# A hand-written issue list in finer words: recurrent attention and a Fourier mixing layer on one core

## The chip, the cores and the metric

The kernel runs on one core of one Trainium2 chip. A core has five engines that work side by side and wait for each other through semaphores: TensorE (PE in the profile; PEld is its loading of weights), VectorE (DVE), ScalarE (ACT), GpSimd (POOL), and SyncE (SP), which here only issues DMA transfers. The metric is device time in microseconds (us). The kernel before took 525.47 us, the median of three runs (524.52, 525.47, 526.28).

## The reference

A gated recurrent attention ("units" are pairs of heads; 4 batches of 8 heads make 16 units) is followed by a two-dimensional Fourier mixing, a normalisation and a two-layer network. Cut to what is computed:

```python
f = 1 / (1 + exp(-f_logit))                      # (4, 8, 768, 48)
for t in range(768):
    state = f[:, :, t, :, None] * state + einsum('bhd,bhe->bhde', k[:, :, t], v[:, :, t])
    y[:, :, t] = einsum('bhd,bhde->bhe', q[:, :, t], state)
x = y.transpose(0, 2, 1, 3).reshape(4, 768, 384)
mixed = real(fft(fft(x, axis=1), axis=2))
u = x + mixed
un = (u - mean(u)) / sqrt(var(u) + 1e-6)         # over the 384 channels
out = u + maximum(un @ w_ch1, 0) @ w_ch2         # 384 -> 1536 -> 384
```

## The kernel before, in words

**Units.** A unit (two heads, both in one tile of 112 rows and 768 tokens) goes through `attention` and `outputs`. The gates are made into running products inside chunks of 128 tokens: two activations on ACT (lines 372 and 373), a scan on DVE (379, tile `W`), two exponentials on ACT (383, 384), and two products on DVE (391 makes q times the decay, 392 makes k over the decay). PE multiplies keys with queries (400, tile `sc`), DVE masks them (404, tile `at`), PE applies them to the values (559, tile `y`) and makes each chunk's state (599, tile `ds`). DVE chains the states with a scan (607, tile `stt`), PE adds their part to `y` (616), ACT takes `y` out, PE turns it (636, tile `yt`), ACT writes it to `x`. `fold` then makes sums and differences of rows on DVE (663 to 669), and after a batch's last unit those of columns (678 to 687), of which `se` (681) is what the first transform reads first.

**Batches.** When the four units of a batch are folded, `fnet` transforms rows (724, tile `z`, against the table `tab`) and columns (743, tile `mix`, against `cd`), adds and normalises (779, tile `un`; 782 turns it with PE). `projected` multiplies by the first weight matrix (871, tile `up`, in batch 0; 840, tile `ub`, with sums of operands that save products, in the others) and by the second (880, tile `po`, once; 894, tiles `fx` and `fz`, elsewhere).

**Weights.** They arrive as 64-bit floats in 24 pieces (`raw`, three buffers). Each is made a 32-bit float by ACT (281), DVE (283, 284) and POOL (285); POOL's step frees the buffer for the next transfer. At the end `judge` looks at the sizes met and decides whether a slow path has to run (962 to 972, with one product on PE, 969).

**What sets the order.** Nothing is scheduled by a planner. `ORDER` is a list of words, and each word issues one step: a number advances that unit's generator to its next `yield`; F, P and H advance a batch's transforms, its projection and its normalisation; L loads a unit's operands; r fetches a piece of weights, C converts one; V and c reread the weights and look at their sizes; B makes a sum of weights; K turns a unit's keys; M is `judge`; D issues eight 128x128 bf16 products into a spare corner of a PSUM tile that nothing reads (`busy`, line 192). Within an engine, instructions run in the order in which the list issues them, and an instruction that waits holds up all that stand behind it on its engine. The list issues D 21 times.

Of the kernel before, what the change touches and what calls it, by code (L numbers as in the profile page):

```python
# [83 lines left out]
def kernel(  # L84
# [280 lines left out]
    def attention(u, x_all):  # L365
# [18 lines left out]
        nc.scalar.activation(W, W, AF.Exp)  # L384
        te = te_t[u % 2][:R]
# [5 lines left out]
        nc.vector.tensor_tensor(Q, Q, g, ALU.mult)  # L391
        nc.vector.tensor_tensor(g, W, K, ALU.mult)
# [149 lines left out]
    def outputs(u, x_all, AT, Q, K, te, T=None):  # L542
# [26 lines left out]
        if te is not None:  # L569
            own, far = AT  # L570
            diagonal(hi, lo)
            ps = ps_a.tile([128, 2, 512], F32, tag="sc", name=f"sc{u}_1")
            for i in range(NCH // 2):
                for p, c in ((0, i), (64, i + 3)):
                    for r in range(2):
                        nc.tensor.matmul(ps[p:p + 64, r, i * 64:i * 64 + 64],
                                         lhsT=K[ROWS[r], c * C:c * C + 64],
                                         rhs=Q[ROWS[r], c * C + 64:(c + 1) * C], start=True, stop=True)
            nc.scalar.copy(far, ps[:, :, :NCH // 2 * 64].rearrange("p r (c t) -> p r c t", t=64))
            yield  # L580
# [6 lines left out]
        else:  # L587
# [4 lines left out]
            diagonal(lo, hi)  # L592
        ps = ps_a.tile([128, 2, 512], F32, tag="sc", name=f"ds{u}")
# [21 lines left out]
        for c, r in ((1, 0), (4, 1), (4, 0), (1, 1), (2, 0), (3, 1), (3, 0), (2, 1), (5, 0), (5, 1)):  # L615
            nc.tensor.matmul(y[ROWS[into(c, r)], c // 3, c % 3 * C:c % 3 * C + C], lhsT=st[ROWS[r], :, c - 1],  # L616
                             rhs=Q[ROWS[r], c * C:(c + 1) * C], start=False, stop=True,
                             skip_group_check=True)

# [15 lines left out]
        for c, i in enumerate((0, 1, 4, 2, 3, 5)):  # L635
            nc.tensor.transpose(ps[:, c * 128:c * 128 + R], to[:, i], ident[:R, :R])  # L636
        x = x_all()
# [9 lines left out]
    def fold(u, x):  # L647
# [16 lines left out]
        tt(f[:, 1:4], x[:, 0:3, ch], x[:, 3:6, ch], ALU.add)  # L664
        tt(f[:, 0:8:7], f[:, 1:7:5], f[:, 2:6:3], ALU.add)
# [13 lines left out]
        if last:  # L679
            eo_of.pop(b)  # L680
            tt(se[:, :, 1:QD], xs[:, :, 1:QD], xs[:, :, HD - 1:QD:-1], ALU.subtract)
            tt(xs[:, :, 1:QD + 1], xs[:, :, 1:QD + 1], xs[:, :, HD - 1:QD - 1:-1], ALU.add)
        tt(xc[:, :, lo:hi], eo[:, 0:4, lo:hi], eo[:, 0:4, up], ALU.add)
# [18 lines left out]
    def fnet(b, x):  # L702
# [71 lines left out]
        def turn(c):  # L774
# [4 lines left out]
            nc.vector.tensor_scalar(un, x[:, c], mv[:, c, 0:1], rstd[:, c:c + 1], ALU.subtract, ALU.mult)  # L779
            pt = ps_f.tile([128, 512], F32, tag="f", name=f"pt{b}_{c}")  # L780
# [4 lines left out]
        def turns():  # L785

            for step in ((0, [3], 3, [4, 5], 2, 5, 1, 4) if b < B - 1 else ([4, 5], 2, 5, [3], 1, 3, 0, 4)):
# [4 lines left out]
                else:  # L792
                    turn(step)
# [3 lines left out]
        for c in range(3):  # L797
            mix = mixed(c)
            nc.vector.tensor_tensor(by2(x[:, c]), rising(mix, NQ), by2(x[:, c]), ALU.add)
            moments(c)  # L800
            deviation(slice(c, c + 1))
            nc.vector.tensor_tensor(by2(x[:, c + 3]), falling(mix, NQ), by2(x[:, c + 3]), ALU.add)
# [311 lines left out]
```

## Time and profile before

| | |
|---|---|
| median of 3 runs | 525.47 us |
| profiled execution, span | 526.3 us (526.257 in the trace) |
| PE busy | 494.9 us, 94% |
| DVE busy | 378.3 us, 72% |
| ACT, POOL busy | 218.4 us, 58.8 us |
| first product of the first transform (line 724) | 59.54 us |
| last piece of weights converted on DVE (line 284) | 117.00 us |
| last product of the program starts and ends | 517.32 us, 519.43 us |

The span is the time from the first to the last instruction of one execution. A row of a timeline gives start, length, engine, line, operation, tiles (out<-in), shape, how many instructions are merged in it, and in brackets the idle time before it with what ended it. PE's busy time has the pipeline's overlap in it, so products are better judged by the distance between their starts.

### The profile page before, as it was taken

The numbers are of one execution on the slowest core, as the hardware profiler recorded it, in microseconds if no ns is written. First come the engines' busy times: TensorE is split into PE (matmuls) and PEld (weight loads), VectorE is DVE, ScalarE is ACT, GpSimd is POOL, SyncE is SP. The second block draws the span as 40 slices with busy tenths as digits, with TensorE's granted clock in tenths as the row PEclk, the third lists the DMA queues.
The fourth block names the chain that finished last, engine by engine and source line by source line (L and its number), as shares of the span: only waits on it lengthen the run. The fifth ranks groups of instructions, "written<-read, shape, count | busy, mean of one in ns | idle before, by whom it ended". The sixth has DMA issues, their size and how long they took to land.

```text
span 526.3 us, 13807 instructions
## 1 busy us (share of the span) xinstructions
PE 494.9 (94%) x5854; PEld 453.4 (86%) x5854; DVE 378.3 (72%) x746; ACT 218.4 (42%) x520; POOL 58.8 (11%) x85
## 2 busy tenths in 40 slices
PE   5878599999999999999999999999999999999994
PEld 4757388866899889999999999999999999999994
DVE  3598989989955368688588776779776667465571
ACT  5567368656331542453435523550431404031220
POOL 3045033551001000000001000000001000010100
PEclk9789699999999999999999999999999999999998
DMA  8957837575010230103212012120610312220200
GB/s 222 268 147 206 210 109 214 161 221 158 6 55 30 68 97 17 54 21 114 77 55 84 1 55 72 46 63 23 206 43 15 107 47 81 83 91 8 84 11 27
DMA packets 20650, 48.15 MB, mean 91 GB/s; under 512 B 3426, under 2 KB 6179, under 8 KB 20579
## 3 DMA queue, kind: packets, MB, share of 16 engines
q1 hardware_dynamic: 19474, 43.63, 29.5%
q0 software_dynamic: 1104, 3.54, 1.8%
q8 instruction: 48, 0.79, 0.6%
q14 instruction: 24, 0.19, 0.1%
HBM read 42.44 MB, written 4.72 MB: 90 GB/s over the span
## 4 chain that ended last, share of the span: by engine, by line
PE 87%; DVE 6%; issue 2%; ACT 2%; DMA 1%; POOL 0%; SPq 0%; DVEq 0%; ACTq 0%
PE ub L840 23%; PE fx L894 16%; PE fz L894 11%; PE up L871 9%; PE z L724 5%; PE y L559 4%; PE mix L743 3%; PE y L616 2%; PE sc L400 2%; PE ds L599 2%; PE po L880 2%; PE yt L636 2%; PE pt L782 1%; PE st L538 1%; PE y L192 1%
## 5 line engine op out<-in xcount | busy, mean ns | idle before, releaser
L849 DVE TENSOR_TENSOR h<-h,ub 128x512 f32<-128x512 f32 x81 | 55.2, 687 | 33.5 <-PE ub L840 24.5
L692 POOL DMA_INDIRECT out_dram<-x,place x16 | 16.4, 1024 | 357.6 <-DVE x L944 224.3
L847 ACT ACTIVATE h<-ub 128x512 f32<-128x512 f32 x54 | 31.9, 591 | 42.3 <-PE ub L840 42.3
L871 PE MATMUL up<-unT,w 128*128 128x256 f32 x216 | 49.4, 382 | 0.0
L840 PE MATMUL ub<-wide,w 128*128 128x128 f32 x360 | 45.0, 276 | 2.3 <-DVE wide L814 2.3
L894 PE MATMUL fx<-block,h 128*128 128x192 f32 x264 | 46.9, 328 | 0.0
L894 PE MATMUL fx<-w,h 128*128 128x192 f32 x264 | 45.5, 327 | 0.0
L840 PEld LDWEIGHTS ub<-wide,w 128*128 128x128 f32 x360 | 42.4, 192 | 3.4 <-PE pt L782 1.3
L871 PEld LDWEIGHTS up<-unT,w 128*128 128x128 f32 x216 | 40.1, 190 | 5.9 <-ACT h L873 0.4
L851 ACT ACTIVATE h<-h 128x512 f32<-128x512 f32 x45 | 28.4, 631 | 38.1 <-DVE h L849 37.7
L894 PEld LDWEIGHTS fx<-block,h 128*128 128x128 f32 x264 | 43.2, 190 | 0.5 <-DVE x L911 0.2
L894 PEld LDWEIGHTS fx<-w,h 128*128 128x128 f32 x264 | 42.7, 190 | 0.4 <-issue 0.2
L285 POOL TENSOR_TENSOR w<-w,raw 128x384 uint32<-128x384 uint32 x24 | 29.4, 1228 | 72.3 <-DVE w L284 39.1
L840 PE MATMUL ub<-unT,w 128*128 128x128 f32 x288 | 37.0, 275 | 0.0
L840 PEld LDWEIGHTS ub<-unT,w 128*128 128x128 f32 x288 | 34.6, 192 | 0.0
L783 ACT COPY unT<-pt 128x384 f32<-128x384 f32 x24 | 11.4, 484 | 46.8 <-PE pt L782 46.6
L840 PE MATMUL ub<-unT,wide 128*128 128x128 f32 x216 | 29.1, 278 | 0.0
L840 PE MATMUL ub<-wide 128*128 128x128 f32 x216 | 28.6, 275 | 0.1
L873 ACT ACTIVATE h<-up 128x256 f32<-128x256 f32 x36 | 13.9, 385 | 33.6 <-PE up L871 22.0
L840 PEld LDWEIGHTS ub<-unT,wide 128*128 128x128 f32 x216 | 26.4, 192 | 0.5
L840 PEld LDWEIGHTS ub<-wide 128*128 128x128 f32 x216 | 26.3, 192 | 0.3 <-PE ub L840 0.3
L379 DVE TENSOR_TENSOR_SCAN W<-g,bound 112x768 f32<-112x768 f32 x12 | 21.0, 1747 | 6.7 <-ACT g L373 6.7
(194 smaller groups left out, 1000.1 us busy)
## 6 DMA issues: line engine op xcount, KB each, us to landing
raw<-in_w_ch_dram SPq DMA_DIRECT2D x24, 384.0 KB, 5.1
v<-in_v_dram SPq DMA_DIRECT2D x16, 288.0 KB
k<-in_w_ch_dram SPq DMA_DIRECT2D x12, 384.0 KB, 3.4
g<-in_w_ch_dram SPq DMA_DIRECT2D x12, 384.0 KB, 3.3
k<-in_qkf_dram SPq DMA_DIRECT2D x14, 288.0 KB
g<-in_qkf_dram SPq DMA_DIRECT2D x12, 288.0 KB, 3.5
q<-in_qkf_dram SPq DMA_DIRECT2D x12, 288.0 KB, 3.3
wide<-in_qkf_dram SPq DMA_DIRECT2D x10, 288.0 KB, 4.7
```

The source lines that it names most:

```text
L285: nc.gpsimd.tensor_tensor(bits, bits, lo, ALU.add)
L379: nc.vector.tensor_tensor_scan(W, g, bound[:R], 0.0, ALU.add, ALU.min)
L559: nc.tensor.matmul(y[FILL[g], c // 3, c % 3 * C + t.start:c % 3 * C + t.stop], lhsT=vals[rows, o:o + (64 if g == 0 else D)], rhs=weights, ...
L692: nc.gpsimd.indirect_dma_start(out=out.rearrange("b s d -> (b s) d"), out_offset=bass.IndirectOffsetOnAxis(ap=place[:, b, i:i + 1], axis=0 ...
L724: nc.tensor.matmul(z[:, cols], lhsT=src[:, j, lo:hi], rhs=tab[:, t, T % 2, cols], start=(i == 0), stop=(i == len(parts) - 1), skip_group_c ...
L743: nc.tensor.matmul(mix[:, o], lhsT=zz[:rows_of[T], T, PLACES[c]], rhs=cd[:rows_of[T], T, :NQ - odd], start=(i == 0), stop=(i == 1))
L840: nc.tensor.matmul(chains[chain][:, m * 128:(m + 1) * 128], lhsT=block(w)[:, m * 128:(m + 1) * 128], rhs=tokens(a), start=(new and m == 0) ...
L847: nc.scalar.activation(out, got, kind, scale=1.0 if how == "=+" else -1.0)
L849: nc.vector.tensor_tensor(out, out, got, ALU.add if how == "+" else ALU.subtract)
L851: nc.scalar.activation(out, out, AF.Relu)
L871: nc.tensor.matmul(pp[:, :256], lhsT=w1[:, kt, m * 128:(m + 1) * 128], rhs=unT[:, kt], start=(kt == 0), stop=(kt == 2))
L894: nc.tensor.matmul(out, lhsT=h[:, m], rhs=blocks[i][:, m], start=(start and m == 0), stop=(m == H - 1), skip_group_check=True)
```

## The change

The list gets finer: 955 words stand in it in place of 720, counted in the text of the two lists. The generators get more `yield`s, so that a step that issued several instructions in one go is cut in two or three: in `attention`, `outputs`, `fold`, `fnet`, `turn` and `hidden`. A unit now takes 19 to 22 words and not 12 or 13, a batch's transforms 13 and not 7, a projection of the batches 1 to 3 32 words a pair and not 23. The words stand in another sequence. D is issued 7 times in place of 21: three ahead of the first unit's products, four later. All other instructions are the same on every engine, in another order; 112 of the 168 spare products are gone.

```diff
 ORDER = (
-    "L0f Z I 0 L0q L2q D D L1f L0k D 0 D 0 i D 1 L2f 2 0 D D D L0v 0 L1k K0 D 0 0 D L1q 0 1 D r 1 L3fk D "
-    "D D L1v 2 0 L2k 1 D r r D 1 2 1 3 3 0 C K1 1 2 0 C 1 L3q 2 1 3 C L2v 2 r K2 L4fk 3 L3v L5fk 1 2 1 D "
+    "L0f 0 I L0q L1f 0 Z i 0 1 0 D 0 L0k 0 L2f 2 L1q D D L1k 1 1 1 0 0 L0v L3fk L2q K0 1 D 0 0 3 1 K1 D 2 "
+    "0 L2k 0 0 r 2 L1v 2 r 2 2 0 1 1 0 K2 1 C 1 1 1 3 C 3 2 1 1 2 1 0 0 L3q 3 L2v 2 2 3 3 1 L4fk 1 0 0 1 "
...
         nc.scalar.activation(W, W, AF.Exp)
+        yield
         te = te_t[u % 2][:R]
...
         nc.vector.tensor_tensor(Q, Q, g, ALU.mult)
+        yield
         nc.vector.tensor_tensor(g, W, K, ALU.mult)
         yield
...
+            yield
             nc.scalar.copy(far, ps[:, :, :NCH // 2 * 64].rearrange("p r (c t) -> p r c t", t=64))
             yield
...
             diagonal(lo, hi)
+            yield
         ps = ps_a.tile([128, 2, 512], F32, tag="sc", name=f"ds{u}")
...
             for i, one, two, sign in made:
                 add(tokens(i), tokens(one), tokens(two), sign)
+            if made:
+                yield
             new = chain not in opened
...
             if complete and not first:
+                yield
                 nc.scalar.activation(out, out, AF.Relu)
             yield
```

The prediction speaks of three places. The first is DVE's queue near the start, from the scan of unit 1 (`W1`) on; `stt0` is unit 0's scan of states, `q1` and `g1` are unit 1's products, `raw0` is the first piece of weights. Before:

```order
L379 SCALAR_TENSOR_TENSOR W1_352<-g1_86,bound_96 112x768
L380 TENSOR_TENSOR deep_97<-g1_86,W1_352 112x6
L379 SCALAR_TENSOR_TENSOR W2_400<-wide_84,bound_96 112x768
L380 TENSOR_TENSOR deep_97<-wide_84,W2_400 112x6
L607 SCALAR_TENSOR_TENSOR stt0_403<-ds0_341,te0_98 112x288
L391 TENSOR_TENSOR q1_90<-q1_90,g1_86 112x768
L392 TENSOR_TENSOR g1_86<-W1_352,k1_88 112x768
L404 COPY_PREDICATED at1_92<-causal_95,sc1_0_429 128x768
L379 SCALAR_TENSOR_TENSOR W3_460<-wide_84,bound_96 112x768
```

And in the changed kernel:

```order
L386 SCALAR_TENSOR_TENSOR W1_195<-g1_86,bound_96 112x768
L387 TENSOR_TENSOR deep_97<-g1_86,W1_195 112x6
L413 COPY_PREDICATED at0_91<-causal_95,sc0_0_201 128x768
L399 TENSOR_TENSOR q1_90<-q1_90,g1_86 112x768
L401 TENSOR_TENSOR g1_86<-W1_195,k1_88 112x768
L386 SCALAR_TENSOR_TENSOR W2_299<-wide_84,bound_96 112x768
L387 TENSOR_TENSOR deep_97<-wide_84,W2_299 112x6
L618 SCALAR_TENSOR_TENSOR stt0_339<-ds0_328,te0_98 112x288
L399 TENSOR_TENSOR wide_84<-wide_84 112x768
L401 TENSOR_TENSOR wide_84<-W2_299,wide_84 112x768
L413 COPY_PREDICATED at1_92<-causal_95,sc1_0_364 128x768
```

Unit 1's products have moved ahead of unit 0's scan of states, and unit 2's (on tile `wide`) have come between that scan and the masking of unit 1.

The second is PE's queue at the same place: the states of unit 0 (`ds0`), their part of `y`, and the key products of unit 1 (`sc1_0`). In the changed kernel they follow each other directly:

```order
L610 MATMUL ds0_328<-v0_227,kT0_243 64x48x2
L610 MATMUL ds0_328<-v0_227,kT0_243 48x48x2
L627 MATMUL y_82<-q0_89,stt0_339 48x128 x10
L409 MATMUL sc1_0_364<-q1_90,g1_86 64x64 x24
L547 MATMUL st2_396<-ident_110,wide_84 128x112 x5
```

Before, six words D with 48 spare products stood between `ds0` and `sc1_0`, and the part of `y` behind `sc1_0`.

The third is DVE's queue at the last pieces of weights (`raw21` to `raw23`). Before, with the normalisation of two token blocks (`un0_2`, `un0_5`) among them:

```order
L283 TENSOR_SCALAR w2_107<-raw21_1680 128x384
L284 SCALAR_TENSOR_TENSOR w2_107<-raw21_1680,w2_107 128x384
L779 TENSOR_SCALAR un0_2_1773<-x0_526,mv0_1096,rstd0_1097 128x384
L283 TENSOR_SCALAR w2_107<-raw22_1702 128x384
L284 SCALAR_TENSOR_TENSOR w2_107<-raw22_1702,w2_107 128x384
L812 SCALAR_TENSOR_TENSOR wide_84<-w1_106 128x512
L283 TENSOR_SCALAR w2_107<-raw23_1724 128x384
L284 SCALAR_TENSOR_TENSOR w2_107<-raw23_1724,w2_107 128x384
L779 TENSOR_SCALAR un0_5_1837<-x0_526,mv0_1096,rstd0_1097 128x384
```

And in the changed kernel:

```order
L290 TENSOR_SCALAR w2_107<-raw20_1646 128x384
L291 SCALAR_TENSOR_TENSOR w2_107<-raw20_1646,w2_107 128x384
L795 TENSOR_SCALAR un0_4_1705<-x0_529,mv0_1000,rstd0_1001 128x384
L618 SCALAR_TENSOR_TENSOR stt7_1707<-ds7_1689,te1_99 112x288
L290 TENSOR_SCALAR w2_107<-raw21_1648 128x384
L291 SCALAR_TENSOR_TENSOR w2_107<-raw21_1648,w2_107 128x384
L290 TENSOR_SCALAR w2_107<-raw22_1650 128x384
L291 SCALAR_TENSOR_TENSOR w2_107<-raw22_1650,w2_107 128x384
L290 TENSOR_SCALAR w2_107<-raw23_1659 128x384
L291 SCALAR_TENSOR_TENSOR w2_107<-raw23_1659,w2_107 128x384
L676 TENSOR_TENSOR eo1_1744<-x1_1441 128x3x96
```

All four of batch 0's remaining normalisations now stand ahead of `raw21`, and so does the scan of unit 7; the last of them and that scan are all that is left between `raw20` and `raw21`, and between `raw21` and `raw23` nothing is left.

More of the change, by code (lines that the diff above doesn't have):

```diff
@@ L664, in fold @@
         tt(f[:, 1:4], x[:, 0:3, ch], x[:, 3:6, ch], ALU.add)
+        yield
         tt(f[:, 0:8:7], f[:, 1:7:5], f[:, 2:6:3], ALU.add)
@@ L679, in fold @@
         if last:
+            yield
             eo_of.pop(b)
@@ L682, in fold @@
             tt(xs[:, :, 1:QD + 1], xs[:, :, 1:QD + 1], xs[:, :, HD - 1:QD - 1:-1], ALU.add)
+            yield
         tt(xc[:, :, lo:hi], eo[:, 0:4, lo:hi], eo[:, 0:4, up], ALU.add)
@@ L779, in turn @@
             nc.vector.tensor_scalar(un, x[:, c], mv[:, c, 0:1], rstd[:, c:c + 1], ALU.subtract, ALU.mult)
+            yield
             pt = ps_f.tile([128, 512], F32, tag="f", name=f"pt{b}_{c}")
@@ L792, in turns @@
                 else:
-                    turn(step)
+                    yield from turn(step)
                 yield
@@ L798, in fnet @@
             mix = mixed(c)
+            yield
             nc.vector.tensor_tensor(by2(x[:, c]), rising(mix, NQ), by2(x[:, c]), ALU.add)
@@ L801, in fnet @@
             deviation(slice(c, c + 1))
+            yield
             nc.vector.tensor_tensor(by2(x[:, c + 3]), falling(mix, NQ), by2(x[:, c + 3]), ALU.add)
@@ L834, in hidden @@
                 add(tokens(i), tokens(one), tokens(two), sign)
+            if made:
+                yield
             new = chain not in opened
@@ L850, in hidden @@
             if complete and not first:
+                yield
                 nc.scalar.activation(out, out, AF.Relu)
@@ L861, in projected @@
             if again:
-                for _ in range((3, 3, 2)[j]):
+                for _ in range((5, 5, 4)[j]):
                     next(behind[b], None)
```

43 rows, old and new, of the table ORDER are left out of this document.

## The prediction

> **What bounds the kernel now.** I read the chain of waits and the clock first, then busy time by stage, then the waits of the engine that sets each stage. Chain, and the granted TensorE clock in 40 slices of 13.2 us:
>
> ```profile
> PEclk9789699999999999999999999999999999999998
> ...
> PE 87%; DVE 6%; issue 2%; ACT 2%; DMA 1%; POOL 0%; SPq 0%; DVEq 0%; ACTq 0%
> ```
>
> TensorE (PE) holds most of the chain, VectorE (DVE) 6%. That average hides three stages. Busy time in them (PE, PEld, DVE, ACT, POOL, each with its instructions, then granted clock, DMA share, GB/s):
>
> ```profile
> core 0: us, PE busy (x) PEld busy (x) DVE busy (x) ACT busy (x) POOL busy (x), PEclk, DMA share, GB/s
> 6.48:58.98 52.50, 37.89 (x925) 32.69 (x922) 41.42 (x67) 33.72 (x73) 13.35 (x20) 0.83 0.85 222
> 58.98:117.56 58.58, 57.07 (x917) 45.22 (x917) 52.30 (x91) 37.36 (x100) 23.10 (x19) 0.94 0.60 172
> 117.56:519.45 401.89, 398.04 (x3997) 373.61 (x3997) 284.21 (x589) 144.28 (x343) 17.50 (x17) 1.00 0.21 62
> ```
>
> From 117.56 on PE is busy 398.04 of 401.89 us at full clock: that stage costs what PE's work costs. In the second stage DVE has 52.30 us of work in 58.58 us. What ends it is the last piece of weights (line 283 and 284), the normalisation behind it on DVE (779), and PE's turning of that block (782), after which the first product by the second weights (880) can run. DVE, then PE:
>
> ```profile
> 116.61 0.36 DVE L283 TENSOR_SCALAR w<-raw 128x384 uint32<-128x384 uint32 x1 [0.96 <-DMA raw<-in_w_ch_dram]
> 117.00 0.56 DVE L284 SCALAR_TENSOR_TENSOR w<-raw,w 128x384 uint32<-128x384 uint32 x1
> 117.48 0.47 DVE L779 TENSOR_SCALAR un<-x,mv,rstd 128x384 f32<-128x384 f32 x1
> ```
>
> ```profile
> 118.10 0.52 PE L782 MATMUL pt<-ident,un 128*128 128x128 f32 x3 [0.57 <-DVE un L779]
> 118.45 2.75 PE L880 MATMUL po<-w,h 128*128 128x384 f32 x8
> ```
>
> I call the end of that pair, 117.56, the gate: behind it, each microsecond by which it moves is one of the whole.
>
> The first stage runs to the start of `se` (681) at 58.98, which the first transform reads. DVE is busy 41.42 of 52.50 us there, and two of its waits are large; the grouped waits of DVE from 6 to 60 us (sum, times, largest), then the timeline around the larger instance of each:
>
> ```profile
> DVE at L404 <- PE sc L400: 4.3, 2, 3.1
> DVE stt L607 <- PE ds L599: 4.2, 2, 2.8
> ...
> 18.74 1.43 PE L599 MATMUL ds<-v,kT 128*64 128x48 f32 x20
> 20.11 4.93 PE L192 MATMUL y<-bound 128*128 128x128 bf16 x48
> 20.23 0.76 DVE L607 TENSOR_TENSOR_SCAN stt<-ds,te 112x288 f32<-112x288 f32 x1 [2.82 <-PE ds L599]
> 21.92 0.96 DVE L392 TENSOR_TENSOR g<-W,k 112x768 f32<-112x768 f32 x1
> 24.97 0.93 PE L400 MATMUL sc<-q,g 48*64 48x64 f32 x48
> 25.96 1.04 DVE L404 COPY_PREDICATED at<-causal,sc 128x768 f32<-128x768 uint32 x1 [3.08 <-PE sc L400]
> ```
>
> DVE has made unit 1's operands (line 392) by 22.88. Then it stands until 25.96, since PE works through 48 spare products until 24.97 before it takes up unit 1's key products.
>
> **The change part by part.** The sum is made against the profiled execution, 526.26 us; the median of the runs is 525.47, so I take 0.8 off at the end.
>
> *A, the first stage.* Work first. Unit 5's scan and the conversion of the fourth piece of weights move behind `se`:
>
> ```profile
> 15.45 1.76 DVE L379 TENSOR_TENSOR_SCAN W<-wide,bound 112x768 f32<-112x768 f32 x1
> 17.24 0.17 DVE L380 TENSOR_TENSOR deep<-wide,W 112x6 f32<-112x6 f32 x1
> ```
>
> By these rows and the pair at 116.61 that is 1.76 + 0.17 + 0.36 + 0.56 = 2.85. Two products of unit 4 move ahead of `se`, 2 x 0.96 = 1.92. Net -0.9. Waits next. In the new order unit 1's products and unit 0's masking stand ahead of unit 0's scan of states, so the 2.82 us in which DVE waited for `ds` is filled with work. On PE the key products stand directly behind `ds` and its part of `y`, so the 3.08 us go too: together -5.9. Against that, fewer spare products mean more work at half clock, as the next rows say: +0.3. A = -0.9 - 5.9 + 0.3 = -6.5. The bounds: -0.9 - 2.1 = -3.0 if only the spare products' own time after 22.88 (to 24.97) is won, and -0.9 - 8.5 = -9.4 if both groups of waits vanish (4.3 + 4.2).
>
> The spare products elsewhere in this stage cost nothing now: PE is busy 37.89 of 52.50 us with them, and the idle 14.6 us cover them. What their removal can cost is the clock, and the trace shows both levels:
>
> ```profile
> 17.70:24.40 6.70, 6.07 (x68) 5.73 (x69) 2.57 (x3) 3.68 (x6) 0.00 (x0) 0.50 1.04 284
> 55.30:65.40 10.10, 5.86 (x14) 3.79 (x15) 9.45 (x22) 3.57 (x11) 0.00 (x0) 0.50 0.76 207
> ...
> 229.07 0.85 PE L599 MATMUL ds<-v,kT 128*64 128x48 f32 x20
> ```
>
> At half clock (0.50) the same 20 products took 1.43 us, and 0.85 at full clock; I take half of that difference, +0.3, since the group may run at either clock. The spare products before were themselves run at half clock (17.70 to 24.40), so they did not keep it up there. The first transform shows the price at its largest:
>
> ```profile
> 58.98 0.46 DVE L681 TENSOR_TENSOR se<-xs 128x285 f32<-128x285 f32 x1
> 59.54 2.85 PE L724 MATMUL z<-tab,se 128*95 128x385 f32 x6 [4.38 <-issue]
> 62.19 2.77 PE L724 MATMUL z<-tab,xs 128*96 128x385 f32 x6
> ...
> 182.13 1.47 PE L724 MATMUL z<-tab,xs 128*96 128x385 f32 x6
> 183.43 1.48 PE L724 MATMUL z<-tab,ce 128*97 128x385 f32 x8
> ```
>
> From start to start one group took 62.19 - 59.54 = 2.65 us there and 183.43 - 182.13 = 1.30 in a later batch: two groups lost 2.7. That loss is in the time before, and I leave it unchanged. The Trainium skill's "TensorE: Matmul & The Clock Gate", in Part 1 on the HAM clock gate, says that the clock is raised after a window of sustained work of about 3.4 us and falls back after an idle one, so that gaps over some 3 us are to be avoided; that speaks against taking spare products away. An estimate from that page's window: a cold start of two windows, 6.8 us, loses at most 3.4 us where 2.7 are lost already, and the sum below would be 0.7 us longer. The trace agrees in kind, with a clock of 0.50 until 65.40, 5.9 us after the transform began.
>
> *B, from `se` to the gate.* DVE's work there, from the rows above and these two:
>
> ```profile
> 119.30 0.74 DVE L607 TENSOR_TENSOR_SCAN stt<-ds,te 112x288 f32<-112x288 f32 x1
> ...
> 114.96 0.69 DVE L812 SCALAR_TENSOR_TENSOR wide<-w 128x512 f32<-128x512 f32 x1
> ```
>
> What A took out comes in here, +0.9. Unit 7's scan of states comes in front of the last pieces, +0.74, and so do the three normalisations that ran behind the last piece, 3 x 0.47 = +1.41; one sum of weights moves behind it, -0.69. Together +2.4. The pieces of weights have three buffers, so a piece can be converted only when the piece three before it has been released by GpSimd (POOL) and the transfer has landed. Two rounds of that loop show as waits, the second in the row at 116.61:
>
> ```profile
> 104.42 0.56 DVE L284 SCALAR_TENSOR_TENSOR w<-raw,w 128x384 uint32<-128x384 uint32 x1
> ...
> 109.26 0.61 DVE L283 TENSOR_SCALAR w<-raw 128x384 uint32<-128x384 uint32 x1 [0.76 <-DMA raw<-in_w_ch_dram]
> 109.90 0.56 DVE L284 SCALAR_TENSOR_TENSOR w<-raw,w 128x384 uint32<-128x384 uint32 x1
> ```
>
> Piece 17's pair ended at 104.98 and piece 20 could start at 109.26: a round of 4.3 us. Piece 20's ended at 110.46 and piece 23 started at 116.61: 6.1 us. In the new order the pieces stand closer. Between 17 and 20 there are 2 x 0.47 for normalisations, 1.04 for a masking and 2 x 0.92 for pieces, 3.8 us; between 20 and 23 0.47 + 0.74 + 2 x 0.92 = 3.1 us. With a round of 5.2, the mean, DVE would wait 1.4 + 2.1 = 3.5 where it waited 0.76 + 0.96 = 1.7: +1.8. The bounds are +0.0 (a round of 4.3: 0.5 + 1.2) and +3.6 (6.1: 2.3 + 3.0). DVE's other waits I leave as they are. B = 2.4 + 1.8 = +4.2, from +2.4 to +6.0.
>
> *C, at the gate.* Before, the normalisation at 117.48 had to pass DVE behind the last pair; now all of them stand ahead of it. The product by the second weights follows the pair itself, as the normalisation did: -0.4, the end of that normalisation, 117.95, less 117.56. If POOL's step on the last piece held the product up instead, it would be 0; if PE also found a turned block waiting, -0.9 (118.45 - 117.56).
>
> *D, behind the gate.* PE work that ran behind the gate now runs ahead of it: unit 7's part of `y`, its turning, and the turning of two blocks of batch 0. A group of each kind, and of the last kind the row at 118.10:
>
> ```profile
> 229.85 0.79 PE L636 MATMUL yt<-ident,yT 112*128 112x112 f32 x6
> 234.49 0.91 PE L616 MATMUL y<-q,stt 48*48 48x128 f32 x20
> ```
>
> 0.79 + 0.91 + 2 x 0.52 = 2.74 by length. A group's length holds the pipeline's overlap with the next one (1.47 against 1.30 from start to start at 182.13), some 0.15 each: 2.1. Ahead of the gate it lies beside DVE's work. Against that, finer words cut units' small products apart: from the last group of line 880 on, the order shows 32 switches from full products to a unit's small ones, 25 before. PE's weight loading sat idle at such places from 65 us on (sum, times, largest):
>
> ```profile
> PEld y L616 <- issue: 2.4, 9, 0.3
> ```
>
> 2.4 / 9 = 0.27 each; 7 x 0.27 = +1.9. D = -2.1 + 1.9 = -0.2. The bounds: -2.1 if the switches are hidden, +3.8 for twice their price with nothing won. The added `yield`s issue nothing themselves.
>
> *E, the end.* The word M (`judge`) stood among the last products, and its product waited on PE:
>
> ```profile
> 505.21 0.38 PE L969 MATMUL turned<-ident,most 128*1 128x128 f32 x2 [0.73 <-DVE most L967]
> 505.62 0.28 DVE L970 TENSOR_REDUCE most<-turned 1x1 f32<-1x128 f32 x1 [0.56 <-PE turned L969]
> ...
> 490.69 1.13 PE L840 MATMUL ub<-wide,w 128*128 128x128 f32 x8 [0.94 <-DVE wide L814]
> ```
>
> It now stands earlier, ahead of the sums of the last pair (814), and 33 words of products follow it where 8 did. DVE's steps of it, this and a shorter one (972), 0.4 in all, then lengthen a wait as the 0.94 at 490.69 for that pair. I take -0.73 + 0.4 = -0.3, with bounds of -0.7 and +0.8 (the steps twice over). The pair waits are otherwise in place, three more of the kind at 0.3 to 0.9: 0, from -2.3 (all covered by the finer words) to +2.3 (doubled).
>
> Sum: -6.5 + 4.2 - 0.4 - 0.2 - 0.3 = -3.2. 526.26 - 3.2 = 523.1 for a profiled execution; less 0.8, **522.3 us**.
>
> **The rivals.** *R1, the weights' loop takes all of it.* Transfers are no faster; if the pieces come as they come now, the gate stays at 117.56. For it: the wait of 0.96 on a transfer right at the gate. Against it: only two such waits, 1.7 us in all. What is left is C, D and E: -0.9, and 0.8 for the median, so 524.6.
> *R2, finer words pay everywhere.* In the last stage PE is idle for 401.89 - 398.04 = 3.9 us; a finer mixture could fill the pair waits (2.3) and hide the switches (1.9). 522.3 - 4.2 = 518.1. With a loop round of 4.3 as well, 516.3. For it: between the small words more products stand ready. Against: the pair wait follows a DVE step that stands where it stood.
> *R3, the other side: the clock stays at half.* The first transform is followed by the second and the weights' first products at full clock from 65.40 on. With 14 words D gone, holes in PE's work between 50 and 70 us could keep 0.50 for longer. Work of some length at full clock then takes twice that, until the slack of PE against DVE in the second stage, 58.58 - 52.30 = 6.3, is used up. With 12 us of such work the gate comes 12 - 6.3 = 5.7 later, 528.0; it decides from 9.5 us on (6.3 + 3.2). For: 0.50 for 10.1 us across the transform already. Against: the second stage's mean of 0.94 leaves no low clock behind 65.40 (6.4 us at 0.50 and the rest at 1.00 give 0.95), and PE's work is dense from there on.
> That the change does not do what it says is ruled out by the orders: the same instructions, but for 112 spare products.
>
> **How the numbers follow.** The forecast has 0.50, R1 0.20, R2 0.18, R3 0.12. The likeliest case's own range is 519.5 to 525. The range, 516.0 to 527.2, takes in R2's 516.3 on one side and R1 with its own spread on the other: some 10 in 100, nearly all R3, lie above and 6 below. About 0.3% is what a measurement of this kernel can tell from no change; that is 523.9 to 527.0. The forecast's case gives 0.42 faster and 0.08 same, R1 0.05 and 0.13 with 0.02 slower, R2 0.18 faster, R3 0.02 same and 0.10 slower. Faster 0.65, same 0.23, slower 0.12.
>
> **What would show it.** A: `se` between 52 and 54 us, the 3.08 wait for `sc` and the 2.82 wait for `ds` gone or under 1; wrong if `se` stays behind 56. B: the last pair (284) ends near 115.5, with waits of DVE for `raw` of some 3.5 us in all; if it ends at 117.5 it is R1, if it ends behind 120 and the clock row shows a fresh 0.50 behind the transform, R3. D: from the gate to the last product 401.5 us, and the idle of PEld before `y` up by 1.9; 398 or less would be R2. E: no wait over 0.3 before `turned`. The forecast is wrong as a whole if the first stage wins less than 3 us.

## The result, and the profile after

The changed kernel took 529.99 us (median of 20 runs, 527.55 to 531.87), the kernel before in the same comparison 526.60 us (20 runs, 524.52 to 529.23). The ratio is 1.0063, with a 95% interval of 1.0046 to 1.0079: slower by 0.6%, where 522.3 us and a gain had been forecast. The profiled execution of the changed kernel has a span of 529.2 us, that of before 526.3.

The clock in 40 slices (13.2 us each) and the share of the engines in the chain of waits, after the change:

```profile
PEclk9969899999999999999997999999999999999998
...
PE 79%; DVE 7%; DMA 7%; ACT 3%; issue 1%; POOL 1%; SPq 1%; POOLq 0%; DVEq 0%; ACTq 0%
```

Two things are new. Transfers are on the chain for 7% where they had 1% (pieces of weights make 3 of the 7, the table of the first transform 2). And in the middle of the stage that ran at full clock throughout, there is a slice with a 7. At the end of the front part the gate stands where it was forecast. DVE near the start (the scan of states, the masking of unit 1, `se`), then the last piece of weights on DVE, then on PE the first transform and the first wait behind the gate, and DVE's wait for pieces of weights from 54 to 116 us:

```profile
21.24 0.76 DVE L618 TENSOR_TENSOR_SCAN stt<-ds,te 112x288 f32<-112x288 f32 x1 [2.59 <-PE ds L610]
...
23.81 1.04 DVE L413 COPY_PREDICATED at<-causal,sc 128x768 f32<-128x768 uint32 x1
...
54.24 0.48 DVE L696 TENSOR_TENSOR se<-xs 128x285 f32<-128x285 f32 x1
...
114.88 0.56 DVE L291 SCALAR_TENSOR_TENSOR w<-raw,w 128x384 uint32<-128x384 uint32 x1
```

```profile
54.82 2.85 PE L740 MATMUL z<-tab,se 128*95 128x385 f32 x6 [1.92 <-POOL cd L254]
...
116.73 1.24 PE L902 MATMUL po<-w,h 128*128 128x384 f32 x3 [0.63 <-POOL w L292]
```

```profile
DVE w L290 <- DMA raw<-in_w_ch_dram: 4.6, 4, 2.0
```

`se` starts at 54.24, 4.7 us earlier than before. The last pair ends at 115.44, 2.1 us earlier (the gate). So the loss arose behind the gate, where it also used up this gain: from there to the end of the last product it is 522.74 - 115.44 = 407.3 us, and 519.43 - 117.56 = 401.9 before, 5.4 us more. (The last product starts at 520.63 and takes 2.11.) The windows behind the gate show where (PE, PEld, DVE, ACT, POOL, granted clock, DMA share, GB/s):

```profile
115.44:273.20 157.76, 157.11 (x1680) 140.41 (x1678) 112.16 (x216) 62.08 (x150) 7.39 (x6) 1.00 0.23 66
273.20:277.60 4.40, 0.00 (x0) 0.00 (x0) 2.50 (x5) 2.25 (x4) 0.00 (x0) 0.86 0.00 1
276.40:283.20 6.80, 5.58 (x17) 5.59 (x18) 4.01 (x13) 2.27 (x4) 0.68 (x1) 0.50 0.00 0
283.30:522.70 239.40, 237.15 (x2265) 227.63 (x2263) 164.56 (x357) 76.13 (x181) 10.08 (x11) 1.00 0.20 62
```

For 157.8 us PE is busy but for 0.7. Then it stands still for 4.4 us, and the 5.6 us of work that follow run at half clock, which costs 2.8 more: 7.2 us. The other 1.8 the remaining stage gave back. The view of each engine's timeline at that place, in the order of cause: SyncE's issues (first the longest wait in its queue between 240 and 280 us), ACT, DVE, PE.

```profile
SPq L219 <- PE sc L585: 17.3, 1, 17.3
...
266.62 0.32 SPq L219 DMA_DIRECT2D g<-in_qkf_dram  x1
...
268.38 0.42 SPq L219 DMA_DIRECT2D g<-in_qkf_dram  x1
```

```profile
270.06 0.84 ACT L379 ACTIVATE g<-g 112x768 f32<-112x768 f32 x1 [6.18 <-DMA g<-in_qkf_dram]
...
273.23 0.84 ACT L379 ACTIVATE g<-g 112x768 f32<-112x768 f32 x1 [0.99 <-DMA g<-in_qkf_dram]
273.98 0.19 ACT L379 ACTIVATION_READ_ACCUMULATOR g<-g 112x1 f32 x1
274.19 0.84 ACT L380 ACTIVATE g<-g 112x768 f32<-112x768 f32 x1
```

```profile
268.01 0.95 DVE L934 TENSOR_TENSOR h<-h 128x768 f32<-128x768 f32 x1
275.07 1.76 DVE L386 TENSOR_TENSOR_SCAN W<-g,bound 112x768 f32<-112x768 f32 x1 [6.11 <-ACT g L380]
276.86 0.17 DVE L387 TENSOR_TENSOR deep<-g,W 112x6 f32<-112x6 f32 x1
276.95 0.35 DVE L957 TENSOR_TENSOR x<-fz,x 128x192 f32<-128x192 f32 x1
277.21 0.35 DVE L960 TENSOR_TENSOR x<-fz,x 128x192 f32<-128x192 f32 x1
```

```profile
271.06 2.11 PE L916 MATMUL fx<-block,h 128*128 128x192 f32 x12
277.62 1.65 PE L916 MATMUL fz<-w,h 128*128 128x192 f32 x4 [4.44 <-DVE x L960]
```

The words at this place are `L14fk 14 10 12 L13fk P1 13 13 13 11 P1 P1 P1`. Unit 14's load can be issued at 266.62 only, when PE has done the products that used its buffer, and unit 13's stands behind it in SyncE's queue, at 268.38. The word `14`, directly behind its load, puts two activations into ACT's queue; ACT waits for the transfer until 270.06. Unit 13's transfer lands after that, at about 273.2. Unit 13's scan has to wait for unit 13's activations, and it stands in DVE's queue ahead of the additions (lines 957 and 960) that take the results out of the PSUM tile `fz`. The products of the last of the four `P1` words are to fill that tile again. ACT waits for a transfer, DVE for ACT, PE for DVE. In the old list unit 13's first gate word stood 39 words behind its load, and `14` eleven words behind its own.

### The profile page after: what moved, and what is told of

It is laid out like the page before. It is cut to its first block, busy times and chain, and to the rows that moved or that the text cites. A ratio compares the mean times of both kernels' runs of the same rounds, so it can differ in the third digit from the quotient of the medians.

```text
span 529.2 us, 13585 instructions
## 1 busy us (share of the span) xinstructions
PE 496.7 (94%) x5742; PEld 452.1 (85%) x5742; DVE 375.8 (71%) x746; ACT 217.7 (41%) x520; POOL 56.1 (11%) x85
## 4 chain that ended last, share of the span: by engine, by line
PE 79%; DVE 7%; DMA 7%; ACT 3%; issue 1%; POOL 1%; SPq 1%; POOLq 0%; DVEq 0%; ACTq 0%
PE ub L861 23%; PE fx L916 16%; PE fz L916 12%; PE up L893 6%; PE z L740 4%; PE y L568 3%; DMA raw<-in_w_ch_dram 3%; PE mix L759 2%; PE sc L409 2%; PE ds L610 2%; DMA tab<-in_seq_tab_dram,back 2%; PE po L902 2%; PE y L627 2%; DMA g<-in_qkf_dram 1%; DVE W L386 1%
## 5 line engine op out<-in xcount | busy, mean ns | idle before, releaser
L893 PE MATMUL up<-unT,w 128*128 128x256 f32 x216 | 51.1, 386 | 0.8 <-ACT h L895 0.6
L292 POOL TENSOR_TENSOR w<-w,raw 128x384 uint32<-128x384 uint32 x24 | 27.9, 1161 | 68.5 <-ACT raw L288 33.8
L916 PE MATMUL fz<-w,h 128*128 128x192 f32 x132 | 25.5, 347 | 4.4 <-DVE x L960 4.4
L916 PEld LDWEIGHTS fz<-w,h 128*128 128x128 f32 x132 | 23.4, 203 | 4.9 <-DVE x L960 4.7
```

Source lines behind the costliest of these rows:

```text
L292: nc.gpsimd.tensor_tensor(bits, bits, lo, ALU.add)
L893: nc.tensor.matmul(pp[:, :256], lhsT=w1[:, kt, m * 128:(m + 1) * 128], rhs=unT[:, kt], start=(kt == 0), stop=(kt == 2))
L916: nc.tensor.matmul(out, lhsT=h[:, m], rhs=blocks[i][:, m], start=(start and m == 0), stop=(m == H - 1), skip_group_check=True)
```

## The experiments

Three theories stood against each other. H: this one late load costs the time, by the idle stretch and the half clock behind it. S: the finer words cost a little everywhere. C: the missing spare products cost it by the clock. The old list is used below in finer words too, cut so that it issues what it issued before. The diffs show only the words around an altered place, not whole lines of the list.

**The place mended.** Unit 13's words stand behind the block that they split:

```diff
-L14fk 14 10 12 L13fk P1 13 13 13 11 P1 P1 P1 11 11 11 P1 P1 12 12 P1
+L14fk 14 10 12 L13fk P1 11 P1 P1 P1 11 11 11 P1 P1 13 13 13 12 12 P1
```

> The changed list with one place altered: unit 13's three gate words stand behind the six P1 words of the block they had split (and behind unit 11's words), not ahead of them. Theory H (a load that lands late holds ScalarE, the scan behind it holds VectorE, and TensorE stands still for 4.4 us and then runs 6.8 us at half clock): the idle stretch of 4.44 us near 277 us goes, the clock shows no 0.50 between 80 and 520 us, and the kernel takes 521 to 524 us, some 7 less than the changed kernel and faster than the kernel before (ratio 0.990 to 0.995). Rival S (the finer words cost a little at many places all through the last stage): less than 2.5 is won, ratio over 1.001. Rival C (the missing spare products leave a low clock that costs the difference): nothing is won, ratio near 1.006.

Measured: 523.64 us, ratio 0.9947 (0.9922 to 0.9972). From slower by 0.6% to faster by 0.5%, 6.4 us, by moving three words. ACT, DVE and PE at the place:

```profile
266.29 0.84 ACT L379 ACTIVATE g<-g 112x768 f32<-112x768 f32 x1 [6.14 <-DMA g<-in_qkf_dram]
...
269.21 0.85 ACT L379 ACTIVATE g<-g 112x768 f32<-112x768 f32 x1
```

```profile
267.81 0.35 DVE L960 TENSOR_TENSOR x<-fz,x 128x192 f32<-128x192 f32 x1
...
273.86 1.75 DVE L386 TENSOR_TENSOR_SCAN W<-g,bound 112x768 f32<-112x768 f32 x1
```

```profile
267.34 2.11 PE L916 MATMUL fx<-block,h 128*128 128x192 f32 x12
269.29 2.11 PE L916 MATMUL fz<-w,h 128*128 128x192 f32 x12
```

ACT waits for unit 14's load as long as before, 6.14 us, and it costs nothing, because DVE's additions no longer stand behind it. Behind the gate the profile of this list has 400.96 us (111.83 to 512.79), 6.3 less than the changed kernel: the 7.2 of the idle stretch and the half clock are gone, and one more wait for a pair's sums (0.95 us) has come in. S and C fall as explanations of the loss.

**Only the clock mended.** Nine words D (72 spare products) in the idle stretch:

```diff
-L13fk P1 13 13 13 11 P1 P1 P1
+L13fk P1 13 13 13 11 P1 P1 D D D D D D D D D P1
```

> The changed list with nine words D (72 spare products) put into the place where TensorE stands still near 273 to 277 us. H: the stretch stays about as long but is busy, the granted clock stays at 1.00, and what half clock took (half of 6.8 us, 3.4) comes back: 526 to 527.5 us, ratio 0.999 to 1.002. S and C: no change beyond 0.5 us, ratio 1.005 to 1.007, as the place is not what costs the time.

Measured: 525.82 us, ratio 0.9997 (0.9971 to 1.0024). PE there, and the window around it:

```profile
270.41 4.18 PE L199 MATMUL y<-bound 128*128 128x128 bf16 x72
274.63 2.22 PE L916 MATMUL fz<-w,h 128*128 128x192 f32 x12
```

```profile
268.00:280.00 12.00, 11.96 (x176) 11.43 (x176) 6.07 (x16) 5.78 (x11) 0.45 (x1) 1.00 0.20 50
```

The stretch is still there (4.18 us of work that nothing reads), the clock stays at 1.00, and 4.2 us come back by the medians, against 6.4 when the stretch itself goes. By the profiles, from the gate to the last product, it is 3.2 against 6.3 (404.07 us here, 407.30 and 400.96 in the other two), and the rows above made it 2.8 of 7.2. With intervals of some 1.3 us to either side of the medians the three do not contradict each other: something near half of the loss, or somewhat more, came from the clock.

**The front alone, and the rest alone.** Two lists joined behind the word that converts the last piece of weights, the last C: up to there one sequence, then all remaining words in the order of the other. Of the first of them, against the changed list:

```diff
-... P0 C r L9fk 7 7 H0 H0 7 6 C C 7 7 C 4 L9qv H0 P0 7 ...
+... P0 C r L9fk 7 7 H0 H0 7 6 C C 7 7 C 6 L8fk P0 L8qv B ...
```

> The changed list up to the word that converts the last piece of weights, and from there on the remaining words in the sequence of the kernel before (cut finer, so the instructions stand as they stood). H: the front part's gain of some 5.5 us at the gate is kept to the end: 520 to 523 us, ratio 0.988 to 0.993. S: the same sign, as the old sequence has the fewer switches. C: no gain, 525 to 529 us, since the spare products are missing in the front part.

> The other half: the sequence of the kernel before up to the word that converts the last piece of weights, with its spare products, then the remaining words in the changed sequence. H: the late load and the idle stretch come back without the gain in front: 530 to 536 us, ratio 1.007 to 1.018, with one idle stretch of 3 to 5 us on TensorE and a granted clock of 0.50 behind it. S: slower too, 528 to 531 us, but without such a stretch. C: 525 to 528 us.

Measured: 522.97 us, ratio 0.9945 (0.9917 to 0.9974), for the new front with the old rest; 536.27 us, ratio 1.0180 (1.0138 to 1.0222), for the old front with the new rest. Of the first, the start of the first transform and the last pair; of the second, the waits of PE:

```profile
51.94 2.85 PE L740 MATMUL z<-tab,se 128*95 128x385 f32 x6 [2.02 <-POOL half L257]
...
111.68 0.56 DVE L291 SCALAR_TENSOR_TENSOR w<-raw,w 128x384 uint32<-128x384 uint32 x1
```

```profile
PE fz L916 <- DVE x L960: 4.9, 1, 4.9
```

The front gained and the rest lost. The first gained 3.3 us by the median where some 5.5 were expected. The second came out just above the expected 530 to 536 us. Its stage behind the gate took 412.3 us in the profile (116.97 to 529.23), 10.4 more than before. The idle stretch of 4.88 us and the half clock behind it explain 7.1 of them; four waits of PE where the two lists meet (117 to 122 us) are 2.0 more. The rest is open.

**Which wait, exactly.** Unit 13's load is moved ahead of unit 12's words; in one kernel that is all, in the other the word `14` moves behind the block as well. Unit 13's words stay inside the block in both.

```diff
-L13qv 12 L14fk 14 10 12 L13fk P1 13 13 13 11 P1 P1 P1 11
+L13fk L13qv 12 L14fk 14 10 12 P1 13 13 13 11 P1 P1 P1 11
```

```diff
-L13qv 12 L14fk 14 10 12 L13fk P1 13 13 13 11 P1 P1 P1 11
+L13fk L13qv 12 L14fk 10 12 P1 13 13 13 11 P1 P1 P1 14 11
```

> Only unit 13's load moved up, unit 14's first word left where it was, ahead of unit 13's. ScalarE takes its instructions in order, so it still stands for unit 14's load until about 270 us of the changed kernel's time, and unit 13's activations follow at once and not after another 1.0 us. H: the idle stretch shrinks by about 1 us, from 4.4 to 3.2 to 3.6, the half clock behind it stays or goes with it: 525 to 529.5 us, ratio 0.998 to 1.006. If unit 13's own transfer were the late one, the stretch would be gone and the time that of the run load_first.

> The changed list with unit 13's load of two operands moved ahead of unit 12's words and of unit 14's load, and unit 14's first word (its two activations on ScalarE) behind the block's P1 words. Unit 13's gate words stay where they were, in the middle of the block. H: what costs is that ScalarE waits for a transfer that could only just have been issued; with unit 13's operands there in time, the idle stretch of 4.4 us goes although the scan still stands in the block: 521 to 524.5 us, ratio 0.990 to 0.996. If it were the scan's own place in VectorE's queue (its length of 1.76 us and what it displaces), 1.5 us of idle time or more would stay and the ratio would be over 0.998.

Measured: 527.87 us, ratio 1.0026 (1.0000 to 1.0052), with the load alone; 521.83 us, ratio 0.9913 (0.9882 to 0.9943), with both. The load alone, PE's wait and ACT:

```profile
PE fz L916 <- DVE x L960: 3.5, 1, 3.5
...
270.50 0.84 ACT L379 ACTIVATE g<-g 112x768 f32<-112x768 f32 x1 [6.30 <-DMA g<-in_qkf_dram]
...
272.58 0.85 ACT L379 ACTIVATE g<-g 112x768 f32<-112x768 f32 x1
```

Both, ACT and DVE:

```profile
264.94 0.85 ACT L379 ACTIVATE g<-g 112x768 f32<-112x768 f32 x1
...
266.83 1.75 DVE L386 TENSOR_TENSOR_SCAN W<-g,bound 112x768 f32<-112x768 f32 x1
```

With its operands there, unit 13 still stood behind unit 14's wait in ACT's queue, and the hole shrank by the 1.0 us of unit 13's own transfer, to 3.47. In this one profile the clock stayed at 1.00 behind it, and the stage behind the gate is 4.1 us shorter than in the changed kernel (403.24 us). The median is lower by 2.1 only; whether the clock fell in other executions is not shown. With unit 14 out of the way, the scan stands in the middle of the block and costs nothing. It is the place of a waiting activation in an engine's queue, not the scan's length. This version beats both kernels, by 4.9 us (0.9%) and 8.2 us.

**What step A was worth by itself.** The old list without the six words D that stood ahead of unit 1's key products:

```diff
-0 1 D r 1 L3fk D D D L1v 2 0 L2k 1 D r r D 1
+0 1 r 1 L3fk L1v 2 0 L2k 1 r r 1
```

> The kernel before with its own list, less the six words D (48 spare products) between unit 0's states and unit 1's key products. It asks what step A was worth by itself. As predicted there: unit 1's key products start some 2 to 4 us earlier, the first transform starts 1.5 to 3 us earlier, and the kernel is 1 to 3 us faster (ratio 0.994 to 0.998). If the spare products paid for themselves by the clock, a new stretch of 0.50 shows between 20 and 60 us, the first transform starts no earlier, and the ratio is 0.999 to 1.004.

Measured: 530.81 us, ratio 1.0086 (1.0055 to 1.0117): slower, where a gain was expected. PE's key products and its first transform, then the window behind the states, in this kernel, and last a window of the kernel before:

```profile
22.60 1.57 PE L400 MATMUL sc<-q,g 48*64 48x64 f32 x45 [2.81 <-issue]
...
61.70 2.85 PE L724 MATMUL z<-tab,se 128*95 128x385 f32 x6 [4.38 <-issue]
...
18.80:32.50 13.70, 10.06 (x200) 8.38 (x197) 9.58 (x12) 6.72 (x17) 1.77 (x2) 0.50 0.69 181
```

```profile
24.50:32.50 8.00, 6.06 (x205) 5.09 (x202) 6.43 (x8) 5.41 (x13) 1.50 (x1) 1.00 0.26 57
```

The key products started at 22.60 in place of 24.97, as step A had it: at 22.50 DVE had unit 1's operands ready. DVE's masking of them came at 24.33 in place of 25.96. But PE had stood idle for 2.81 us and the clock was at 0.50 until 32.5, so that the products took 1.57 us in place of 0.93; and the first transform came 2.2 us later. Where between 24 and 61 us that lead was lost is open. Half of the six words were then left in:

```diff
-0 1 D r 1 L3fk D D D L1v 2 0 L2k 1 D r r D 1
+0 1 D r 1 L3fk D D L1v 2 0 L2k 1 r r 1
```

> The list of the kernel before, less three of the six words D between unit 0's states and unit 1's key products (the run no_six took all six away and lost 4 us, with TensorE idle for 2.81 us there and the clock at 0.50 for 13.7 us in one stretch). If the six words paid by bridging that idle stretch, 24 products (2.5 us at half clock, by the 4.93 of 48) bridge most of it and hold the key products up less: the clock is back at 1.00 before 28 us in the profile, and the time is 522.5 to 526.5 us, ratio 0.994 to 1.000. If it takes the whole number of them, the clock stays low as in no_six: 528 to 531 us, ratio 1.004 to 1.009.

Measured: 528.42 us, ratio 1.0035 (1.0006 to 1.0064): the loss of the second reading, at its lower edge, but with the clock of the first. Key products and first transform:

```profile
21.94 0.99 PE L400 MATMUL sc<-q,g 48*64 48x64 f32 x45 [1.37 <-issue]
...
59.77 2.85 PE L724 MATMUL z<-tab,se 128*95 128x385 f32 x6 [4.38 <-issue]
```

In that execution the clock was up and the key products early, and still the first transform started no earlier than before. That the six words paid in the old list is shown; that it was by the clock alone is not. In the new list the same six words were put back (on top of the version with both moves):

```diff
-0 L2k 0 0 r 2 L1v 2 r 2 2 0 1
+0 L2k 0 D D D D D D 0 r 2 L1v 2 r 2 2 0 1
```

> The list of the run load_first with the six words D put back between unit 0's states and its part of y, which unit 1's key products follow. The run no_six showed that in the old list these six words were worth 4 us, by the clock. If they are worth the same in the new list, it gets faster: 518 to 520.5 us, and the clock is at 1.00 from 25 us on in the profile. If the new sequence has put work in their place, they cost their own time and the wait behind them: first transform 2 to 4 us later, 522.5 to 525.5 us, ratio 0.993 to 0.998.

Measured: 525.03 us, ratio 0.9984 (0.9955 to 1.0013), 3.2 us more than that version without them, as the second reading had it. The first transform:

```profile
58.47 2.85 PE L740 MATMUL z<-tab,se 128*95 128x385 f32 x6 [3.13 <-POOL half L257]
```

It started at 53.31 in the version without them. The two lists have the same words behind the gate, and their profiles the same time there, 399.54 us without the six words and 399.52 with them; the gate itself moved from 113.71 to 117.57. So leaving them out is a loss of 4 us in the old sequence and a gain of 3 in the new one, whose order puts unit 0's part of `y` and unit 1's key products in their place. Three words D elsewhere, into smaller idle stretches of the first 30 us, on top of the first mended list:

```diff
-0 L2k 0 0 r 2 ... C 1 1 1 3
+0 L2k 0 D 0 r 2 ... C 1 D D 1 1 3
```

> The changed list with the place at 277 us mended (as in the run apart) and three words D more: one behind unit 0's states and two ahead of unit 1's products with the values, where TensorE was idle for 0.87, 0.62 and 0.77 us. In the changed kernel's trace the clock was 0.50 from 27.2 to 37.4 us, in the run apart it was not. If those idle stretches are what lets the clock fall in part of the executions, the times draw together at the lower end: median 521.5 to 523, ratio 0.990 to 0.993. If the three words only take TensorE's time: 524 to 525.5, ratio 0.996 to 0.999.

Measured: 523.93 us, ratio 0.9956 (0.9932 to 0.9979), against 523.64 without: nothing won, and no cost that could be told from the spread.

**The tail, and the first transform's clock.** The new front with the old rest, and from the first word P3 on the changed list again (but for one V, which the old rest has already issued); then the same with four words D ahead of the first transform:

```diff
-... V c c P3 P3 P3 P3 P3 P3 P3 P3 P3 P3 M P3 P3 P3 P3 P3 P3 P3 P3
+... V c c V c P3 P3 P3 P3 P3 P3 P3 P3 P3 M P3 P3 P3 P3 P3 P3 P3 P3 ...
```

```diff
-3 K4 D 5 5 S F0
+3 K4 D 5 5 S D D D D F0
```

> The run new_then_old with the changed list's sequence again from the first word P3 on, so that the word M stands 33 words ahead of the end and its product finds nothing to wait for. Step E said -0.3 for this, from -0.7 to +0.8; the traces of the runs so far say -1.1 between the last 50 us of work and the end. Expected: no wait of TensorE ahead of the product of line 991, and 521.2 to 523 us, ratio 0.989 to 0.994, against 522.97 for new_then_old. If the new place of M costs as much at the pair's sums as it saves, 522.5 to 524.

> The run best_tail with four words D more directly ahead of the first transform, where TensorE waits 1.2 to 2.6 us for the tables and the clock is low. If the low clock at the first transform still sets the time, the clock row shows 1.00 across it and 1 to 2 us are won: 519.5 to 521 us. If the second stage is set by VectorE and the weights' loop as step B has it, the first transform gets faster or later by 1 us without moving the end: within 0.5 us of best_tail.

Measured: 522.29 us, ratio 0.9920 (0.9889 to 0.9952), and 522.98 us, ratio 0.9924 (0.9897 to 0.9951). PE at `judge` in the first, and the first transform in the second:

```profile
486.25 0.38 PE L991 MATMUL turned<-ident,most 128*1 128x128 f32 x2
...
487.84 1.16 PE L861 MATMUL ub<-wide,w 128*128 128x128 f32 x8 [1.21 <-DVE wide L833]
```

```profile
58.13 1.49 PE L740 MATMUL z<-tab,se 128*95 128x385 f32 x6
```

`judge`'s product waits for nothing, and the sums of the pair behind it wait 1.21 us where they waited 0.94. The medians differ by 0.7 us from the list with the old tail, within their spread. In the second the first transform ran at full clock, its first two groups 1.33 us apart from start to start and not 2.64, and the median is not lower. Step B would have it so, as the stage behind would not be set by PE. But the spare products also held the transform up: it started 2.5 us behind `se` (55.61) where it had been 0.7 (54.05 and 54.77). What full clock alone would bring there is not shown.

## Why the prediction was wrong, point by point

**What bounds the kernel** was right as far as the gate: a microsecond there is one at the end. The two lists with and without the six words show it: gates 3.9 us apart, the same 399.5 us behind them, medians 3.2 us apart. That the last stage "costs what PE's work costs" was right for the old order only, as the step that failed shows.

**A** (-6.5, from -3.0 to -9.4) measured -4.7 in the profile of the changed kernel. Six of the other lists have its words up to the gate (the two with unit 13's or 14's words moved out, the load alone, only the clock, the new front with the old rest, and that with the new tail); in the seven profiles `se` started between 51.32 and 54.63, which is -4.4 to -7.7. The wait of 3.08 for `sc` went in the changed kernel, and at most 1.7 of it was left in the other six. The wait for `ds`, which was to go, stayed at 2.59 (1.0 to 3.2 in the seven): the scan of states still came up before PE had made the states. Wrong was the reason given for the largest part: that taking 48 spare products away frees their time. In the old sequence it cost 4 us. The sentence that the spare products "did not keep it up there" was read from the stretch in which they ran; behind that stretch the clock was at 1.00 in the one profile, and without them, in the other, it was not. The gain comes from the new sequence, in which putting them back costs 3.

**B** (+4.2, from +2.4 to +6.0) measured +2.6: from `se` to the end of the last pair the changed kernel took 61.20 us, the kernel before 58.58. DVE's work grew by 1.7 (53.98 us against 52.30), its waits for pieces of weights by 2.9 (4.6 against 1.7, where 3.5 had been worked out from the loop of three buffers). Its other waits there, which B had left as they were, shrank by 2.0. In the seven profiles B is +1.7 to +3.2. So the gate moved by -2.1, where A and B together said -2.3, because two errors of some 1.7 us cancelled in this execution; that was luck. In the seven it moved by -1.5 to -5.7.

**C, D and E** (-0.9 together): what is left behind the gate without the hole is 5.4 - 7.2 = -1.8. In the first mended list it is 400.96 - 401.87 = -0.9, in the second 399.54 - 401.87 = -2.3. (The 401.5 us that the prediction names as a sign of D do not follow from its own terms, which give 401.9 - 0.9 = 401.0.) At the gate itself PE waited 0.6 us for POOL's step on the last piece, which C had named as what would make it 0. E is the difference between 0.94 + 0.73 before and 1.21 after, -0.5, where -0.3 was said. The switches between full and small products do not show as a loss: the first mended list and the one with the old rest differ by 0.7 us.

**The step that failed** is none of the five. It is the sentence "the pair waits are otherwise in place", and the rivals: everything behind the gate was taken as PE's work, cut into finer pieces, with waits only at the pairs. Loads of operands were not looked at there. The change had put two loads and their first users side by side, and what stands behind a waiting activation on ACT, and then behind the scan on DVE, was not followed. The term for it in the sum was nothing. The runs showed a stretch of 4.44 us in which PE stood still and 2.8 us lost to the half clock behind it. That is 7.2 us in the profile and 6.4 to 8.2 by the medians of the mended lists, which bring it to 521.8 and 523.6 us, around the 522.3 that had been forecast. R3 had the right sign by a wrong mechanism: no clock stayed low behind the first transform.

## What to carry to other kernels

Where a change reorders work by hand, look in the new order for every transfer's first user, with what has to be finished before the transfer can be issued, and then follow the queue behind that user, engine by engine, to the one that bounds the stage; a wait of 6 us on ACT cost nothing or 7 us, by what stood behind it. A hole on TensorE can cost more than its length: 4.44 us of it cost 7.2. And what filler work is worth is not a property of the filler: the same six words saved 4 us in one sequence and cost 3 in another.

## What the runs showed of the hardware

Idle stretches on PE of 4.44 and 4.88 us in the middle of dense work were each followed by a granted clock of 0.50 (the changed kernel, and the old front with the new rest); one of 3.47 us (the load moved alone) was followed by none in the profiled execution. The windows around the second and the third:

```profile
282.30:289.10 6.80, 4.46 (x14) 4.46 (x15) 4.96 (x13) 2.27 (x4) 0.00 (x0) 0.50 0.00 0
```

```profile
273.50:290.00 16.50, 13.03 (x162) 11.90 (x163) 12.54 (x32) 6.57 (x17) 1.95 (x2) 1.00 0.21 66
```

The Trainium skill's "TensorE: Matmul & The Clock Gate", Part 1 on the HAM clock gate, puts the limit at one idle window of about 3.4 us and calls the window free-running, so that the number of slow products varies from run to run. The traces do not contradict it: the two stretches with a fall are longer than that, and a window whose start does not depend on the program need not lie wholly inside a stretch of 3.47. Three stretches do not show where the limit lies.

In the front part the clock differs between executions of the same words. The changed kernel and the first mended list are the same up to some 250 us, yet from 27.2 to 37.4 us the one's profile has 0.50 and the other's 1.00. The changed kernel first:

```profile
27.20:37.40 10.20, 9.69 (x192) 8.32 (x196) 7.38 (x14) 4.40 (x12) 1.98 (x2) 0.50 0.91 245
```

```profile
27.20:37.40 10.20, 8.21 (x307) 6.96 (x300) 9.53 (x20) 7.25 (x18) 2.31 (x2) 1.00 0.99 250
```

The first transform came at 54.82 and 52.13 us. So one profile of the front part is one draw, and the times of one kernel spread over 4 us and more. The spread goes with the clock: of 90 executions of the kernel before that ran beside the experiments, the 21 with a mean granted clock of 0.983 or more have a median of 524.9 us, the 30 with 0.977 or less one of 527.9. Which of the two brings the other about is not shown.
